# Products of nothing ahead of the first join of four groups, in a fused RWKV-7 and top-k expert kernel

## The chip, the cores and the metric

The kernel runs on one core of a Trainium2 chip. Its time is the device time of one execution in microseconds (us); the figure given for a kernel is the median of several executions. The profile is of one execution; its span runs from the first to the last instruction on the core.

## What is computed

An RWKV-7 recurrence over 768 steps, for 4 batches of 8 heads of width 40, and behind it a mixture of 8 experts that keeps the best 80 tokens of each expert.

```python
for t in range(S):                                    # S = 768
    y[:, :, t] = np.einsum('bhd,bhde->bhe', rt, state)
    Sa = np.einsum('bhde,bhe->bhd', state, at)
    state_decay = state * wt[:, :, None, :] - np.einsum('bhd,bhe->bhde', Sa, bt)
    state = state_decay + np.einsum('bhd,bhe->bhde', vt, kt)
# x: (3072, 320) from y
logits = x @ w_gate                                   # 8 experts
# each expert keeps its `capacity` = 80 tokens of the largest gate weight
h = np.maximum(x[tok_idx] @ w1[e], 0.0)
out[tok_idx] = gate_w[tok_idx, None] * (h @ w2[e])
```

## The kernel before

The 768 steps are cut into 12 chunks of 64, and the batches into 2 pairs: 24 units of work. A unit is prepared (`prepare`: loads, transposes, running products, scores), its triangular system is inverted, and it is finished (`finish`: the values, the state update, the output rows). Units 0 to 3 are inverted on TensorE by repeated squaring (`doubling`). From unit 4 on four units form a group, `batches[1]` to `batches[5]`: units 4 to 7, 8 to 11, 12 to 15, 16 to 19, 20 to 23. `invert` writes a group's scores to DRAM (`blocks`), fetches them into a layout in which GpSimd (POOL) solves all the 32-row diagonal blocks of the group at once (lines 677 and 679, 30 steps), writes the solutions and their transposes back (`solved`, `flipped`, line 697), and SyncE (SP) loads these into the tiles `d1` (line 706), `nt` (line 713) and `d0` (line 719).

`solve` joins the 32-row blocks of one unit to 64-row blocks with two sets of eight small products on TensorE: `g_go` multiplies `nt` and `d0` (line 737; called G below), ScalarE (ACT) copies the result to `gt` (line 742), `x_go` multiplies `gt` and `d1` (line 752; called X), and ACT copies that back into `nt` (line 757). G of the first unit of a group waits for that group's loads.

After that the unit's `finish` runs: `u_go` (line 875) and `ut_go` (line 894) on TensorE, copies on ACT (880, 900), the masked product `lam` (line 811, masked on VectorE, DVE, at line 818 into `UL`), then the large products of `keys_go` (line 930) that give state and output. `gate` works out the gate weights of a group, writes rows to DRAM (`x_rows`, line 1048), turns the gate weights on TensorE (line 1063) and keeps the ten times eight largest so far with pairs of DVE instructions (lines 1056 and 1058, ten rounds).

The order of the work is written by a planner. Every operation is handed over with `add(engine, duration, lag, when, function, reads, writes, psum)`, and `Plan.order` lists all of them by a simulated clock; each engine then executes its own list strictly in that order. The planner also places the results of TensorE in the eight banks of PSUM (`bank(key)` gives the place). G is handed over as an operation of 0.6 us. A DMA of the hardware queues takes one of eight semaphores by turns, so one that is issued later can wait for an earlier one on its semaphore.

When all units are through, the 80 best are known, token numbers are worked out from them, the rows are gathered and the experts run in six passes (`first_layer`, `second_layer`). In that part there are already products of nothing, `keep_warm` at line 1173, seven of 384 columns.

Of the kernel before, what the change touches and what calls it, by code (L numbers as in the profile page):

```python
# [17 lines left out]
class Plan:  # L18
# [7 lines left out]
    def add(self, eng, us, lag, when, fn, reads=(), writes=(), psum=None, to=()):  # L26
        whole = eng == "PE" and psum[0][0] in WHOLE
        o = dict(eng=eng, us=us, lag=lag, when=when, stage=self.stage, fn=fn, whole=whole, i=len(self.ops), deps=set(), psum=None,
                 reads=list(reads), writes=list(writes), to=list(to))
        if psum:  # L30
            key, n = psum
            if key not in self.width:
                self.width[key] = n
                o["psum"] = key
            o["writes"].append(key)
        o["kind"] = f"{eng} {(psum[0] if psum else [*o['writes'], *o['reads'], ('none', 0)][0])[0]}"
        for key in o["reads"]:
            for p, wrote in self.touch.get(key, ()):
                if wrote:
                    o["deps"].add(p)  # L40
        for key in o["writes"]:
            for p, _ in self.touch.get(key, ()):
                o["deps"].add(p)
        for key in o["reads"]:
            self.touch.setdefault(key, []).append((o["i"], False))
        for key in o["writes"]:
            self.touch.setdefault(key, []).append((o["i"], True))
        self.ops.append(o)
# [140 lines left out]
def kernel(  # L189
# [19 lines left out]
    nc = tc.nc  # L209
# [25 lines left out]
    batches = [list(range(n, n + GU)) for n in range(0, NM, GU)]  # L235
# [11 lines left out]
    ident = const.tile([128, 128], F32, name="ident")  # L247
# [25 lines left out]
    def view(t, offset, *dims):  # L273
        return bass.AP(t.tensor, t.offset + offset, [list(t.ap[0])] + [list(d) for d in dims])
# [28 lines left out]
    with ExitStack() as p1:  # L303
        hold = p1.enter_context(tc.tile_pool(name="hold", bufs=1))
        psp = p1.enter_context(tc.tile_pool(name="psp", bufs=1, space=PSUM))
        ps = psp.tile([128, 8, 512], F32, name="ps")
# [8 lines left out]
        begins = hold.tile([128, H * SEG], F32, name="begins")  # L315
# [13 lines left out]
        def at(name, n):  # L329
            return buf[name][n % RINGS[name]]  # L330

        def group(name, n):
            return wide[name][(n // GU) % WIDE[name]]

        def quads_of(name, n, rows=slice(0, 128)):
            return group(name, n)[rows].rearrange("p (q u i t) -> p u q i t", q=2, u=GU, t=T)[:, n % GU]

        def bank(key):
            return plan.home[key]
# [290 lines left out]
        def invert(kq):  # L630
# [93 lines left out]
            add("SP", 0.8 * 2 * len(qs), 2.6, z + 5, d0_go, [("flp", kq)], [("d0", n) for n in ns])  # L724
            add("SP", 0.8 * 2 * len(qs), 3.2, z + 5, nt_back_go, [("sol", kq)], [("nt", n) for n in ns])

        def solve(n):
            z = n * PER

            kg, kx = ("G", n), ("X", n)  # L730

            def g_go():
                b0 = bank(kg)
                nt, d0 = quads_of("nt", n), quads_of("d0", n)
                for i in range(M4):
                    for q in range(2):
                        nc.tensor.matmul(ps[HB * q : HB * q + HB, b0, T * i : T * i + T], lhsT=nt[:, q, i, :],
                                         rhs=d0[:, q, i, :], start=True, stop=True, skip_group_check=True)
            add("PE", 0.6, 0.3, z - 8, g_go, [("nt", n), ("d0", n)], (), (kg, 1), [("gt", n)])

            def gt_go():
                nc.scalar.copy(at("gt", n).rearrange("p (c t) -> p c t", t=T)[:, :, 0:C],
                               ps[:, bank(kg), 0:256].rearrange("p (c t) -> p c t", t=C))
            add("ACT", 0.4, 0.1, z - 7, gt_go, [kg], [("gt", n)])

            def x_go():
                b0 = bank(kx)
                gt = at("gt", n).rearrange("p (i x t) -> p i x t", x=2, t=T)
                d1 = group("d1", n).rearrange("p (u i x c) -> p u i x c", u=GU, x=2, c=T)[:, n % GU]
                for i in range(M4):  # L750
                    for x in range(2):
                        nc.tensor.matmul(ps[T * x : T * x + T, b0, T * i : T * i + T], lhsT=gt[:, i, x, :],
                                         rhs=d1[:, i, x, :], start=True, stop=True, skip_group_check=True)
            add("PE", 0.6, 0.3, z - 6, x_go, [("gt", n), ("d1", n)], (), (kx, 1), [("nt", n)])

            def tm_go():
                nc.scalar.copy(quads_of("nt", n)[:, :, :, C:],
                               view(ps[:, bank(kx), :], 0, (C, 2), (T, M4), (1, C)))
            add("ACT", 0.4, 0.1, z - 5, tm_go, [kx], [("nt", n)])
# [334 lines left out]
        for kq, ns in enumerate(batches):  # L1094
            plan.stage = (ns[-1] >= 2 * GU) + (ns[-1] == NM - 1)
            for n in ns:
                prepare(n)
            if kq:
                invert(kq)
            for n in ns:  # L1100
                if kq:
                    solve(n)
                finish(n)
                if n == groups[group_of[n]][-1]:
                    gate(group_of[n])
# [58 lines left out]
    with ExitStack() as p2:  # L1164
# [35 lines left out]
        for m0 in range(0, NM, CH):  # L1200
# [3 lines left out]
            for m in range(m0, m0 + CH):  # L1204
                nc.tensor.matmul(ip, lhsT=hot[:, m - m0, :], rhs=ids[:, m].rearrange("p i e -> p (i e)"),
                                 start=m == 0, stop=m == NM - 1)
# [3 lines left out]
        for i, n in enumerate((HB, C)):  # L1210
            for j in range(128 // n):
                nc.tensor.matmul(spread[n * j : n * j + n, i].rearrange("p i e -> p (i e)"),
                                 lhsT=ident[0:HW, HB * i : HB * i + n], rhs=i0, start=True, stop=True, skip_group_check=True)
# [133 lines left out]
```

## Time and profile before

| | us |
|---|---|
| median of 3 executions | 568.6 |
| lowest and highest | 563.7 and 569.66 |
| the profiled execution | 569.61 |
| its span | 567.5 |
| TensorE (PE) products busy / weights loading | 454.1 / 371.6 |
| VectorE (DVE) busy | 339.3 |
| GpSimd (POOL) busy | 222.8 |
| ScalarE (ACT) busy | 208.8 |
| mean granted clock of TensorE | 0.921 of full |

In the profile a line such as "L737" is a line of the kernel before. A row of the timeline gives the start and length in us of a run of equal instructions, its engine and line, what it writes and reads, and in brackets how long the engine stood idle ahead of it and what ended that. An fp32 product is two matmul instructions. PEclk is the clock that TensorE was granted, as a share of full speed.

The recurrence ends at about 467 us. The first joins of the five groups start at 167.6, 235.4, 303.1, 369.6 and 423.4 us.

### The profile page before, as it was taken

To read this page: it belongs to the slowest core of one execution; us is meant where nothing else is said; L and a number is where in the kernel's file an instruction comes from. 1 tells how busy PE (TensorE), PEld (TensorE's weight loads), DVE (VectorE), ACT (ScalarE), POOL (GpSimd) and SP (SyncE) were. 2 spreads that over 40 slices of the span, in tenths; PEclk is the share of its full clock that TensorE was granted. 3 is DMA by queue.
4 is the path that set the end of the run, shared out by engine and by line. 5 is a ranking of instruction groups with operands and counts; after the bars stand their busy time and mean duration, and the time that the engine had idled before them with its cause. 6 is when DMAs were issued, how large, how long until landed. Compare 5 with 4: busy or idle time off the path is not lost. (4 is left out here: it accounts for less than half of the span.)

```text
span 567.5 us, 28199 instructions
## 1 busy us (share of the span) xinstructions
PE 454.1 (80%) x12677; PEld 371.6 (65%) x12677; DVE 339.3 (60%) x752; ACT 208.8 (37%) x424; POOL 222.8 (39%) x412
## 2 busy tenths in 40 slices
PE   2868888689889998699985999399829860799996
PEld 2767777678778887588874988388828750434442
DVE  6879777265363895487663786374377688621211
ACT  1445465346533454245542455234314320021010
POOL 7000001895408982598404986388400000120101
PEclk9999999889987999789997899779968995599999
DMA  7645658433595658856687544832591539289600
GB/s 132 115 73 86 102 102 137 80 75 76 110 176 107 118 94 182 175 98 120 153 146 142 90 92 110 167 53 46 131 188 40 186 100 331 73 241 351 235 13 17
DMA packets 239392, 71.81 MB, mean 127 GB/s; under 512 B 216520, under 2 KB 233928, under 8 KB 239272
## 3 DMA queue, kind: packets, MB, share of 16 engines
q1 hardware_dynamic: 218360, 51.15, 45.5%
q10 hardware_dynamic: 18176, 9.19, 6.3%
q0 software_dynamic: 2736, 9.67, 5.1%
q8 instruction: 99, 1.62, 1.1%
q14 instruction: 21, 0.17, 0.1%
HBM read 52.11 MB, written 16.72 MB: 121 GB/s over the span
## 5 line engine op out<-in xcount | busy, mean ns | idle before, releaser
L677 POOL TENSOR_TENSOR tmp<-lt 128x30 f32<-128x30 f32 (+9 forms) x150 | 80.2, 534 | 34.5 <-DMA lt<-blocks 23.4
L679 POOL TENSOR_TENSOR lt<-lt,tmp 128x30 f32<-128x30 f32 (+9 forms) x150 | 86.6, 577 | 11.7
L661 POOL DMA_DIRECT2D lt<-blocks x5 | 2.9, 586 | 129.9 <-PE ps L437 79.9
L604 PE MATMUL ps<-slot,kbT 40*64 40x64 f32 x1536 | 34.7, 224 | 8.4 <-issue 4.9
L604 PEld LDWEIGHTS ps<-slot,kbT 40*64 40x64 f32 x1536 | 29.0, 136 | 12.1 <-issue 6.3
L543 DVE TENSOR_TENSOR_SCAN slot<-dec,begins 128x520 f32<-128x520 f32 x24 | 31.6, 1317 | 4.6 <-POOL cand L345 3.4
L930 PE MATMUL ps<-UL,slot 64*64 64x128 f32 x768 | 30.0, 293 | 2.3 <-DVE UL L818 1.9
L930 PE MATMUL ps<-VL,slot 64*64 64x128 f32 x768 | 27.8, 272 | 4.8 <-issue 4.7
L818 DVE TENSOR_TENSOR UL<-ps,mask 128x512 f32<-128x512 f32 x24 | 16.5, 688 | 24.8 <-PE ps L811 24.7
L551 DVE TENSOR_TENSOR_SCAN iv<-dec,ends 128x520 f32<-128x520 f32 x24 | 30.9, 1286 | 0.7
L973 DVE TENSOR_TENSOR xT<-ps,slot 128x512 f32<-128x512 f32 x24 | 16.5, 688 | 22.9 <-PE ps L930 22.9
L783 ACT COPY VL<-rawv 128x320 f32<-128x320 f32 x24 | 11.0, 459 | 50.3 <-PE ps L930 41.4
L437 PE MATMUL ps<-ident,slot 128*128 128x128 f32 x192 | 28.6, 297 | 0.9 <-issue 0.8
L593 ACT COPY kbT<-ps 128x1024 f32<-128x1024 f32 x24 | 24.4, 1015 | 13.3 <-PE ps L437 12.2
L1303 POOL DMA_INDIRECT out_dram<-y,idx_s x6 | 6.0, 994 | 57.3 <-DVE y L1302 57.3
L794 ACT COPY rv<-ps 128x1024 f32<-128x1024 f32 x24 | 24.3, 1013 | 10.7 <-PE ps L437 10.7
L1039 POOL TENSOR_TENSOR ids<-gsm,tok 128x32 bf16<-128x32 f32 (+1 forms) x14 | 3.0, 231 | 63.9 <-DVE gsm L1029 43.3
L624 DVE TENSOR_TENSOR slot<-ps,mask 128x512 f32<-128x512 f32 x24 | 16.4, 685 | 17.5 <-PE ps L604 17.5
L930 PEld LDWEIGHTS ps<-VL,slot 64*64 64x64 f32 x768 | 22.3, 135 | 6.8 <-issue 6.8
L985 PE MATMUL ps<-wsel,xT 128*128 128x88 f32 x192 | 25.8, 277 | 1.1 <-DVE xT L973 1.0
L930 PEld LDWEIGHTS ps<-UL,slot 64*64 64x64 f32 x768 | 23.3, 143 | 4.8 <-DVE UL L818 2.7
L985 PEld LDWEIGHTS ps<-wsel,xT 128*128 128x128 f32 x192 | 23.3, 191 | 2.5 <-DVE xT L973 1.5
(216 smaller groups left out, 1143.8 us busy)
## 6 DMA issues: line engine op xcount, KB each, us to landing
w<-in_moe_w_dram SPq DMA_DIRECT2D x4, 1280.0 KB
slot<-in_moe_w_dram SPq DMA_DIRECT2D x4, 1120.0 KB, 7.8
slot<-in_moe_w_dram SPq DMA_DIRECT2D x4, 1024.0 KB, 8.3
w<-in_moe_w_dram SPq DMA_DIRECT2D x4, 1024.0 KB, 11.9
x_rows<-xg ACTq DMA_DIRECT2D x24, 160.5 KB, 3.5
rawk<-in_k_dram SPq DMA_DIRECT2D x48, 80.0 KB, 3.0
raww<-in_w_dram SPq DMA_DIRECT2D x48, 80.0 KB, 3.1
rawr<-in_r_dram SPq DMA_DIRECT2D x48, 80.0 KB, 3.0
```

The costliest lines, as they stand in the source:

```text
L437: nc.tensor.matmul(o, lhsT=i, rhs=ident, start=True, stop=True, is_transpose=True, skip_group_check=True)
L543: nc.vector.tensor_tensor_scan(at("P", n), at("dec", n)[:, 0 : H * SEG], begins, 0.0, op0=Alu.mult, op1=Alu.add)
L551: nc.vector.tensor_tensor_scan(at("iv", n)[:, H * SEG : 0 : -1], at("dec", n)[:, H * SEG : 0 : -1], at("ends", n)[:, H * SEG : 0 : -1], 0. ...
L593: nc.scalar.copy(at("kbT", n).rearrange("p (k c) -> p k c", k=2), ps[:, bank(kk) : bank(kk) + 2, :])
L604: nc.tensor.matmul(ps[T * o : T * o + T, b0 + q, T * i : T * i + T], lhsT=at("kbT", n)[rows, 512 * x + c : 512 * x + c + T], rhs=at("ah", ...
L677: e.tensor_tensor(out=tv, in0=t3[:, 0:s, s : s + 1].to_broadcast([np_, s, n]), in1=t3[:, s : s + 1, s + 1 :].to_broadcast([np_, s, n]), op ...
L679: e.tensor_tensor(out=t3[:, 0:s, s + 1 :], in0=t3[:, 0:s, s + 1 :], in1=tv, op=Alu.add)
L794: nc.scalar.copy(at("rv", n).rearrange("p (k c) -> p k c", k=2), ps[:, bank(kr) : bank(kr) + 2, :])
L818: nc.vector.tensor_tensor(out=view(at(name, n), 512, (HB, 2), (2 * HB, 4), (1, T)), in0=view(ps[:, bank(key), :], 0, (512, 2), (T, 4), (1, ...
L930: nc.tensor.matmul(ps[HB * q : HB * q + HB, b0 + bb, 128 * i : 128 * i + 128], lhsT=at("kb", n)[rows, o : o + HB], rhs=view(at(name, n)[ro ...
L973: nc.vector.tensor_tensor(out=view(at("xT", n), 0, (T, 2), (128, M4), (1, T)), in0=view(ps[:, bank(ky), :], HB, (512, 2), (128, M4), (1, T ...
L985: nc.tensor.matmul(ps[:, b0, o : o + 88], lhsT=at("xT", n)[:, 128 * i : 128 * i + 128], rhs=wsel[:, i, :], start=True, stop=True, skip_gro ...
```

## The change

Ahead of the first G of the groups `batches[2]` to `batches[5]` (units 8, 12, 16 and 20) the kernel issues 3, 6, 10 and 8 products of 512 columns. Each multiplies the identity by the first 512 columns of the constant tile `begins` (zeros, with a one in every 65th column) and writes the bank that this G then overwrites. They are inside `g_go`, so the planner does not know of them and its order stays.

```diff
+        FILL = {batches[2][0]: 3, batches[3][0]: 6, batches[4][0]: 10, batches[5][0]: 8}
+
         def solve(n):
...
             def g_go():
                 b0 = bank(kg)
+                for _ in range(FILL.get(n, 0)):
+                    nc.tensor.matmul(ps[:, b0, :], lhsT=ident, rhs=begins[:, 0:512], start=True, stop=True, skip_group_check=True)
                 nt, d0 = quads_of("nt", n), quads_of("d0", n)
```

## The prediction

> **What bounds the kernel now.** I read the share of busy time first (TensorE 454 of 567.5 us), then TensorE's list of waits (us in total, times, longest), since the change touches nothing else.
>
> ```profile
> PE ps L737 <- DMA d<-flipped: 18.9, 3, 9.7
> PE thr_p L1180 <- DVE thw L1178: 11.9, 1, 11.9
> PE ps L737 <- DMA d<-solved: 8.2, 1, 8.2
> ```
>
> Two of TensorE's three longest waits are G, the line ahead of which the products go: 18.9 + 8.2 = 27.1 us in four waits. The timeline of TensorE gives the four places:
>
> ```profile
> 235.44 1.12 PE L737 MATMUL ps<-d,spare_nt 128*64 128x64 f32 x16 [3.26 <-DMA d<-flipped]
> 303.07 1.12 PE L737 MATMUL ps<-d,nt 128*64 128x64 f32 x16 [5.94 <-DMA d<-flipped]
> 369.58 1.12 PE L737 MATMUL ps<-d,spare_nt 128*64 128x64 f32 x16 [9.68 <-DMA d<-flipped]
> 423.42 1.12 PE L737 MATMUL ps<-d,nt 128*64 128x64 f32 x16 [8.16 <-DMA d<-solved]
> 425.00 1.19 PE L752 MATMUL ps<-d,gt 128*64 128x64 f32 x16
> 429.70 0.69 PE L752 MATMUL ps<-d,gt 128*64 128x64 f32 x16
> ```
>
> These are units 8, 12, 16 and 20. The last two rows are the same work, X, five us apart: 1.19 us and 0.69 us. The clock explains it, in the view of chosen windows (bounds, length, busy us and count of PE, PEld, DVE, ACT, POOL, then PEclk, DMA share, GB/s):
>
> ```profile
> 235.30:245.30 10.00, 8.17 (x167) 7.12 (x169) 3.76 (x12) 1.95 (x6) 8.62 (x18) 0.50 0.83 160
> 300.10:306.80 6.70, 3.73 (x38) 3.31 (x40) 1.39 (x6) 1.17 (x3) 2.29 (x9) 0.50 0.78 122
> 307.00:310.00 3.00, 2.60 (x117) 2.16 (x113) 0.93 (x2) 0.50 (x2) 2.53 (x7) 1.00 0.53 115
> 361.60:375.10 13.50, 5.46 (x115) 4.81 (x116) 4.34 (x19) 1.54 (x4) 9.60 (x24) 0.50 0.81 158
> 416.20:429.70 13.50, 6.19 (x117) 5.14 (x117) 10.50 (x37) 1.97 (x5) 0.00 (x0) 0.50 0.73 126
> ```
>
> The clock falls to half in or just behind each wait and stays there after G has begun: until about 245.4, 306.9, 375.2 and 429.8. So each group pays twice: for the wait, which the products don't shorten, and for 10.0, 3.8, 5.6 and 6.4 us of half speed behind it. The loop of a group is a chain of latencies through TensorE (POOL itself waits for `blocks` 50.1 us in all), so time gained behind a join is passed on: the loads of the next group are issued behind work that TensorE paces.
>
> [...] only 0.50 and 1.00 stand in windows inside a state, and the stretches above are about 10.2, 6.8, 13.7 and 13.7 us long[...]. [...] The products here are plain ones of the identity with a mostly zero operand; the kernel has such products already, at L1173:
>
> ```profile
> 491.40:494.50 3.10, 3.10 (x13) 1.85 (x10) 2.43 (x15) 0.00 (x0) 1.07 (x1) 0.50 0.00 0
> 494.80:497.20 2.40, 2.35 (x8) 1.08 (x6) 0.00 (x0) 0.09 (x1) 1.95 (x2) 1.00 0.51 137
> ```
>
> Nothing else ran on TensorE from 491.5 to 494.6, and the clock rose[...].
>
> **The change part by part.** *Cost of a product.* The groups by line give the length of one matmul, least first:
>
> ```profile
> L1173 PE MATMUL idle<-at,ident x14: 486/589/1009, 486.5 to 496.7; 128*128 128x384 f32 x14
> L1270 PE MATMUL hp<-slot,xe x64: 592/592/643, 498.5 to 518.6; 128*64 128x512 f32 x32, 128*32 128x512 f32 x32
> ```
>
> At full clock 128 columns more cost 592 - 486 = 106 ns, 0.83 ns a column; 512 columns occupy 0.425 us. A product is two instructions: 0.85 us at full clock, 1.70 at half. So 3, 6, 10 and 8 products take 2.55, 5.1, 8.5 and 6.8 us.
>
> *Do they fit?* They wait only for the last reader of their bank. By the program's semaphores that is ACT's copy L846 for unit 8 (ended 231.5), an older copy L539 for unit 12, DVE's L862 for unit 16 (359.10 + 0.49 = 359.6), nothing for unit 20. So they start when TensorE falls idle: about 232.0, 297.1, 359.8 and 415.2, and end at 234.6, 302.2, 368.3 and 422.0, ahead of G by 0.8, 0.9, 1.3 and 1.4 us. Added cost at full clock: nothing, hidden in the wait. [...]
>
> *What is gained.* Warm, the first G takes 0.62 us to the next instruction instead of 1.05 (262.79 to 263.41 against 423.42 to 424.47), X the same, L875 0.49 instead of 0.87, L894 about 0.6 instead of 1.03. By group, following the queue:
>
> - Unit 8: G and L604 behind it would be 0.9 us faster, but X then waits for `d1`, whose first two loads had landed and the others landed at about 239.5. The idle time that this leaves (236.8 to 239.6) is 2.8 us[...]. I take 0; at most 1.3 us (UL at DVE L818 waited 0.64 us for TensorE, and the rounds of DVE ahead of it would start 0.7 earlier).
> - Unit 12: 0.43 of G, 0.86 of the eight transposes behind it (304.13 to 306.02, warm 1.03). ACT's copies and the issue of `x_rows`, for which the next `gt` waits, move along. 1.2 us, at least 0.3 if that issue is held by its DMAs.
> - Unit 16: TensorE alone would gain 2.0. But `d1` landed at 371.05, so X starts no earlier than that; and DVE has eight rounds of gate weights ahead of UL:
>
> ```profile
> 371.15 0.29 DVE L1066 COPY cand<-ps 128x128 f32<-128x128 f32 x1 [8.75 <-PE ps L1063]
> 377.22 0.69 DVE L818 TENSOR_TENSOR UL<-ps,mask 128x512 f32<-128x512 f32 x1 [0.48 <-PE ps L811]
> ```
>
> UL waited for TensorE only 0.48 us, and the rounds start 0.58 us earlier (G 0.43, the transpose L1063 0.15). DVE is late next: 1.06 us.
> - Unit 20: the transpose L1071 behind G waits for DVE's rounds, which end at 424.4 whatever TensorE does; from there L1071, X (`d1` landed at 424.8), L1077, G, L875 and L894 run warm: X of unit 21 at about 427.5 instead of 429.70. DVE's UL waited 1.17 us and the rounds ahead of it start 0.8 earlier: 1.97 at most. I take 1.9.
>
> The sum is 0 + 1.2 + 1.06 + 1.9 = 4.2 us. The other engines' lists are unchanged. At the end of the recurrence DVE's last rounds and TensorE are a near tie (the gate reduction at 468.31 follows the tenth round), but these rounds are themselves started by TensorE's earlier unit, so the gain passes.
>
> **To the time.** The profiled execution took 569.6 us: 569.6 - 4.2 = 565.4. It lies 1.0 above the median of 568.6, so for a median I say 564.4.
>
> **The rivals.**
>
> *Everything comes back.* Unit 8 also stays warm and neither DVE nor `d1` binds. Half-speed work behind the joins, at 42% saved: about 5.8, 3.8, 5.6 and 6.4 us, 21.6 x 0.42 = 9.0, so 559.6. [...] Against it: DVE's 0.48 us of slack at unit 16 is in a fixed order.
>
> *The clock falls anyway.* The remaining gaps of 0.8 to 1.4 us, the wait for `d1` and the DVE wait that replaces the old one [...] drop the clock again a little later. For it: a gap of 1.84 us at 309.7 to 311.6, [...] was followed by half clock from 313.7 to 317.1. Against it: gaps of about 1.1 us (273.4, 411.7) were not. It gives 568 to 568.6.
>
> *Products that outlast the wait (slower).* If the clock is half when they begin, a product takes 1.70 us. [...] The point from which it decides is 0.8 to 1.4 us of lost work, that is 1.6 to 2.8 us at half clock. [...] If the clock never rose, 5.1, 10.2, 17.0 and 13.6 us against waits of 3.3, 5.9, 9.7 and 8.2 would add 18.8: 587.4.
>
> **How the numbers follow.** The forecast gets 0.53, everything back 0.13, the clock that falls anyway 0.22, products that outlast 0.12. The forecast's own range is 562.5 to 567 (2 to 6 us of gain). The three executions before spread over 6 us, so the range reaches to the first rival below and takes in the second: 559.5 to 569.5. About 1% is what a measurement of this kernel can tell from no change. Faster by more than that means below 562.9: most of the first rival and the lower edge of the forecast, 0.22. Slower means above 574.3, the tail of the last rival: 0.06. The rest, 0.72.
>
> **What would show it.** In the changed profile TensorE's waits ahead of G shrink to about 1 us each, and PEclk reads 1.00 where it was 0.50 behind units 12, 16 and 20; G there takes 0.69 us instead of 1.12. Behind unit 16 UL waits for DVE's own rounds and TensorE for UL by about 1 us. Unit 8 keeps a stretch at half clock behind its wait for `d1`. The forecast is wrong if G starts straight behind its last product (they outlast the load), if the distance between the first joins of two groups does not shrink by 1 us or more from unit 12 on, or if half clock merely moves.

## The result, and the profile after

| | before | after |
|---|---|---|
| median of 22 executions each, us | 567.37 | 570.42 |
| lowest and highest | 561.14 and 574.9 | 565.14 and 579.35 |
| the profiled execution / its span | 569.61 / 567.5 | 569.11 / 567.0 |
| mean granted clock | 0.921 | 0.940 |

Ratio after to before 1.0075, 95% interval 1.0047 to 1.0102: slower by 0.75% in this set of runs, where a gain of 4.2 us was forecast. The ratios given here compare, for each kernel, only those runs that lie within 1.5% of its own fastest; as the runs of one kernel spread over 2 to 3%, what that leaves out depends on their number, so I set the difference of the plain means over all runs beside it, with its standard error (here +3.5 +- 1.1 us).

Nothing in the profile looks slower at first. In the page of the changed kernel (engine, busy us, share, instructions; then the clock in tenths by slices of 14.2 us; then a DMA queue with packets, MB and share):

```profile
PE 476.3 (84%) x12731; PEld 380.8 (67%) x12731; DVE 341.7 (60%) x752; ACT 208.6 (37%) x424; POOL 223.6 (39%) x412
PEclk9999999899988998999998999999999875599999
q8 instruction: 100, 1.64, 1.2%
```

The 22 us by which TensorE is busier are the products, and the clock is higher (0.940 against 0.921). The line numbers of the changed kernel are 4 higher from G on: the products are L737, G is L741, `lam` L815 with its mask at L822, `keys_go` L934, the turn of the gate weights L1093. TensorE's timeline at the four joins:

```profile
230.01 2.74 PE L737 MATMUL ps<-begins,ident 128*128 128x512 f32 x6
234.09 0.69 PE L741 MATMUL ps<-d,spare_nt 128*64 128x64 f32 x16 [1.34 <-DMA d<-flipped]
...
294.01 5.42 PE L737 MATMUL ps<-begins,ident 128*128 128x512 f32 x12
299.36 0.69 PE L741 MATMUL ps<-d,nt 128*64 128x64 f32 x16
...
364.34 0.69 PE L741 MATMUL ps<-d,spare_nt 128*64 128x64 f32 x16 [1.30 <-DMA d<-flipped]
...
415.94 0.69 PE L741 MATMUL ps<-d,nt 128*64 128x64 f32 x16 [0.83 <-DMA d<-solved]
```

This is what the prediction promised. The waits of 3.3, 5.9, 9.7 and 8.2 us have become 1.3, none, 1.3 and 0.8, every G takes 0.69 us, and from unit 8's G to unit 20's it is 181.9 us (415.94 - 234.09) instead of 188.0. Unit 20's G starts 7.5 us earlier than before (2.6 of these were there at unit 4 already, ahead of the change). At the end of the span 0.5 us of them is left. The list of waits (us in total, times, longest) has one kind that the prediction did not price:

```profile
PE ps L934 <- issue: 7.3, 6, 2.7
PE ps L947 <- issue: 3.2, 2, 1.7
PE ps L741 <- DMA d<-flipped: 2.6, 2, 1.3
PE ps L815 <- issue: 2.6, 1, 2.6
PE ps L741 <- DMA d<-solved: 0.8, 1, 0.8
```

The list of before has it too, for instance in this row (L930 is the changed kernel's L934):

```profile
PE ps L930 <- issue: 5.0, 4, 2.4
```

"issue" is time in which TensorE had no operand to wait for. In all it is not more than before (26.2 against 27.1 us); what changed is where it falls. Behind the last join the changed kernel has two stops of over 2.5 us (2.70 and 2.58), where before has one of 2.42. The timeline of TensorE and of DVE, first before:

```profile
454.98 0.77 PE L930 MATMUL ps<-VL,slot 64*64 64x128 f32 x19 [2.42 <-issue]
461.30 0.67 DVE L818 TENSOR_TENSOR UL<-ps,mask 128x512 f32<-128x512 f32 x1
464.39 0.21 PE L943 MATMUL ps<-rv,sT 40*64 40x64 f32 x1 [1.04 <-issue]
470.44 0.38 PE L1089 MATMUL ps<-ident,gates 128*8 128x128 f32 x2 [3.00 <-DVE gates L1034]
```

Then after:

```profile
436.10 0.33 PE L934 MATMUL ps<-UL,slot 64*64 64x128 f32 x2 [2.70 <-issue]
458.52 0.49 PE L815 MATMUL ps<-rv,uT 40*64 40x64 f32 x7 [2.58 <-issue]
459.14 0.69 DVE L822 TENSOR_TENSOR UL<-ps,mask 128x512 f32<-128x512 f32 x1 [2.80 <-PE ps L815]
468.94 0.59 PE L1093 MATMUL ps<-ident,gates 128*8 128x128 f32 x2 [3.00 <-DVE gates L1038]
```

The last `UL` is the mark. Before, DVE took it up without a wait, so the stop of 2.42 us had been made good; after, DVE stands 2.80 us for `lam`, which is broken in two by a stop (25 matmul instructions, then seven at 458.52). And the clock, which had been full there, falls. The chosen windows (bounds, length, busy us and count of PE, PEld, DVE, ACT, POOL, then PEclk, DMA share, GB/s), one row of before and three of after:

```profile
429.90:470.60 40.70, 31.00 (x1072) 27.75 (x1070) 31.44 (x94) 13.13 (x32) 0.78 (x4) 1.00 0.44 130
```

```profile
436.10:444.00 7.90, 7.90 (x164) 7.51 (x165) 3.21 (x10) 2.39 (x7) 0.39 (x2) 0.57 0.33 94
444.10:457.60 13.50, 9.91 (x349) 8.45 (x348) 8.65 (x25) 3.43 (x8) 0.00 (x0) 1.00 0.54 165
457.60:464.60 7.00, 4.61 (x87) 4.02 (x86) 4.30 (x11) 0.00 (x0) 0.00 (x0) 0.51 0.02 4
```

From unit 20's G to the last turn of the gate weights ("the last stretch" below) before took 470.44 - 423.42 = 47.0 us, after 468.94 - 415.94 = 53.0. That is where 6 of the 7.5 us went; 1.0 more went between that turn and the first expert product (28.1 and 29.1 us), which I did not follow up. Of the 6, the stops for issue account for 2.6 (6.5 us in the stretch against 3.9). The other 3.4 go with the clock, which was at half for 14.8 us of the stretch instead of 6.3; how much of them the half clock cost is not measured.

**Where the stops come from.** The queue q8 ("instruction" in the page) brought 99 packets before and 100 after, 1.64 MB: 16.4 KB each. The trace of the changed kernel has 12,731 matmuls, as many weight loads and 146 other TensorE instructions, 25,608 in all: 256 to a packet. So I take each packet to bring TensorE a block of 256 instructions. Half a block's instructions are matmuls, so block ends should come every 128 matmuls. They do: in every trace of this case in which weights are loaded early, the stops for issue of over 1 us behind the last join fall at the same place of the count of TensorE's matmuls, modulo 128 (35 or 36): ahead of them stand 11556 and 12067 matmuls after (and 11811 at a stop of 0.83 us), 11811 and 12067 before. Not every block comes in time: of the 26.2 us that TensorE stood for issue, 23.0 end 2 to 3 us behind the beginning of a q8 packet, and one stop took 2.7 us. In most of the last stretch a packet begins some 10 to 80 matmuls into a block, so that the next one is there in time, and at full clock two packets are 3.4 to 4.5 us apart. The packet that ends the stop at 436.10 began at 433.68, 7.2 us behind the one ahead of it, when TensorE had already used up its block, and as a transfer of early weights of 1,120 KB, issued at 428.1, came to its end; so did the one at 456.22, 6.8 us behind its predecessor, with 1,120 KB issued at 451.0. In each case TensorE went on some 2.4 us after the packet began.

The change's 27 products add 54 matmuls and 54 weight loads ahead of the tail. That moves which matmul a block begins with. This is theory A: the loss is the place of the block ends in the last stretch, under bursts of weights, not the time of the products.

### The profile page after: what moved, and what is told of

It reads as the page before. It is cut to its first block, busy times and chain, and to the rows that moved or that the text cites. A ratio compares the mean times of both kernels' runs of the same rounds, so it can differ in the third digit from the quotient of the medians.

```text
span 567.0 us, 28307 instructions
## 1 busy us (share of the span) xinstructions
PE 476.3 (84%) x12731; PEld 380.8 (67%) x12731; DVE 341.7 (60%) x752; ACT 208.6 (37%) x424; POOL 223.6 (39%) x412
## 3 DMA queue, kind: packets, MB, share of 16 engines
q8 instruction: 100, 1.64, 1.2%
## 5 line engine op out<-in xcount | busy, mean ns | idle before, releaser
L677 POOL TENSOR_TENSOR tmp<-lt 128x30 f32<-128x30 f32 (+9 forms) x150 | 84.4, 562 | 33.8 <-DMA lt<-blocks 22.7
L679 POOL TENSOR_TENSOR lt<-lt,tmp 128x30 f32<-128x30 f32 (+9 forms) x150 | 82.8, 552 | 11.8
L934 PE MATMUL ps<-UL,slot 64*64 64x128 f32 x768 | 30.1, 287 | 7.6 <-issue 5.4
L543 DVE TENSOR_TENSOR_SCAN slot<-dec,begins 128x520 f32<-128x520 f32 x24 | 33.7, 1404 | 4.6 <-POOL cand L345 3.1
L604 PEld LDWEIGHTS ps<-slot,kbT 40*64 40x64 f32 x1536 | 29.1, 139 | 10.8 <-issue 4.7
L822 DVE TENSOR_TENSOR UL<-ps,mask 128x512 f32<-128x512 f32 x24 | 16.5, 689 | 25.2 <-PE ps L815 24.9
L934 PE MATMUL ps<-VL,slot 64*64 64x128 f32 x768 | 30.0, 285 | 1.9 <-issue 1.9
L934 PEld LDWEIGHTS ps<-UL,slot 64*64 64x64 f32 x768 | 23.2, 141 | 10.8 <-issue 7.0
L1043 POOL TENSOR_TENSOR ids<-gsm,tok 128x32 bf16<-128x32 f32 (+1 forms) x14 | 3.0, 233 | 66.8 <-DVE gsm L1033 42.5
L624 DVE TENSOR_TENSOR slot<-ps,mask 128x512 f32<-128x512 f32 x24 | 16.5, 686 | 17.1 <-PE ps L604 17.1
L934 PEld LDWEIGHTS ps<-VL,slot 64*64 64x64 f32 x768 | 24.1, 142 | 2.6 <-issue 2.4
L947 PE MATMUL ps<-rv,sT 40*64 40x64 f32 x768 | 23.1, 226 | 3.2 <-issue 3.2
```

The source lines that it names most:

```text
L543: nc.vector.tensor_tensor_scan(at("P", n), at("dec", n)[:, 0 : H * SEG], begins, 0.0, op0=Alu.mult, op1=Alu.add)
L604: nc.tensor.matmul(ps[T * o : T * o + T, b0 + q, T * i : T * i + T], lhsT=at("kbT", n)[rows, 512 * x + c : 512 * x + c + T], rhs=at("ah", ...
L624: nc.vector.tensor_tensor(out=at("psi", n).rearrange("p (q i t) -> p q i t", q=2, t=T), in0=quads(kp).rearrange("p q (i t) -> p q i t", t= ...
L677: e.tensor_tensor(out=tv, in0=t3[:, 0:s, s : s + 1].to_broadcast([np_, s, n]), in1=t3[:, s : s + 1, s + 1 :].to_broadcast([np_, s, n]), op ...
L679: e.tensor_tensor(out=t3[:, 0:s, s + 1 :], in0=t3[:, 0:s, s + 1 :], in1=tv, op=Alu.add)
L934: nc.tensor.matmul(ps[HB * q : HB * q + HB, b0 + bb, 128 * i : 128 * i + 128], lhsT=at("kb", n)[rows, o : o + HB], rhs=view(at(name, n)[ro ...
```

## The experiments

In the expectations, theory A is this one; the rivals are described in each (C is not the same in all of them). Times of kernels are compared only within one set of runs, in which before was timed too.

**Instructions without work, at the start.** Small bf16 products (about 30 ns each) ahead of everything else:

```diff
+        for _ in range(54):            # pad54; 64 in pad64, 128 in pad128; 74 and 10 ahead of the changed kernel
+            nc.tensor.matmul(ps[0:32, 7, 0:32], lhsT=ones_b[:, 0:32], rhs=ones_b[:, 0:32], start=True, stop=True, skip_group_check=True)
```

`pad54` is before with the change's 108 instructions; `after_pad74` is the changed kernel brought to 148 + 108 = 256.

> The kernel before with 54 small bf16 products (108 instructions, as many as the change adds) at the very start, where TensorE still waits for its first loads; none ahead of a join. Theory A (the change moves the places at which TensorE stops for its next block of 256 instructions, at 433.4 and 455.9 us for 2.7 and 2.6 us in the changed kernel, and there the clock falls): the late part of the list has the same shift as with the change, so these stops come at the same instructions and the time is 0.4 to 1.2% over before. Theory B (the products themselves cost: they outlast the loads, or their work lowers the clock later): no difference, within 0.2%. Theory C (the gain arrives and is lost at the end to the weights' transfers, because the end comes earlier): no difference, within 0.2%.

> The changed kernel with 74 small bf16 products at the start: 148 instructions and the 108 of the change are 256, one whole block, so behind the last group the blocks end at the same instructions as in the kernel before. Theory A: the gain of the joins shows, 0.5 to 1.3% faster than before. Theory B: 0.5 to 1.0% slower than before, as the changed kernel. Theory C: 0.3 to 1.0% slower, as the changed kernel.

`pad54`: 581.82 us against 573.82 of before, ratio 1.0155 (1.0057 to 1.0253). `after_pad74`: 573.50, ratio 0.9976 (0.9929 to 1.0024), so its difference to before is gone, the last stretch takes 47.1 us again and its stops are before's (2.22 and 1.31 us, both at before's products). The places of the stops are for A; the gain of 0.5 to 1.3% that A wanted on top is not there. And `pad54` lost more than the change itself, so three further kernels were to control it: one whole block, half a block, and half a block with the change.

> The kernel before with 128 small bf16 products (256 instructions, one whole block) at the start. In the trace of the run with 54 such products TensorE was through with them at 2.9 us, ahead of its first loads at 7.2. Theory A (what counts is where blocks of 256 instructions end): the ends lie where they lie before, so within 0.4% of before, and stops of over 0.6 us fall at the same products. A rival (such products at the start cost by themselves, a warmer clock early or a later start): slower by 1.5% or more, as 54 of them were.

> The kernel before with 64 small products (128 instructions, half a block) at the start. It is the base for the next kernel; theory A says only that it differs from before, between 0.5% faster and 1.6% slower, with its stops half a block away from those of before.

> The changed kernel with 10 small products at the start: 20 and 108 instructions, again half a block, so behind the last group the blocks end as in the kernel with 64. Theory A with a gain of its own in the joins: 0.4 to 1.0% faster than the kernel with 64 small products. Theory D (the joins' waits are set by transfers, the warm clock only makes the next wait longer, no gain of its own): within 0.2% of it.

> The changed kernel once more, beside the others on this chip: 0.5 to 1.0% slower than before, as measured; it ties this chip to the first comparison. Against the kernel with 54 small products, at the same ends of blocks behind the last group (1.0155 of before): 0.4 to 1.0% faster by theory A with a gain of its own, equal by theory D.

Against before at 573.60: `pad128` 580.42 and `pad64` 580.59 (four runs each: +4.7 +- 3.6 and +6.7 +- 2.6 us), `after_pad10` 574.67 (20 runs, 1.0067, 1.0019 to 1.0115; by plain means +0.6 +- 1.2), the changed kernel again 575.98 (four runs, +1.3 +- 2.0). `after_pad10` lies 6.1 +- 2.5 us below `pad64`, at the same block ends: for a gain of the products' own, and against rival D, but on four runs of `pad64`. `pad128` is a miss for A, which had it within 0.4% of before: its two longest stops are where before has them, but the last stretch takes 51.1 us and the median is 1.2% higher, though four runs that lie between 568.72 and 583.51 cannot tell its time from before's. Whether padding at the start has a price of its own in the first 170 us I did not settle: unit 4's G starts at 172.3 to 175.0 us in before with padding (`pad54`, `pad64`, `pad128`) and at 167.6 in before, but kernels untouched there show 165.0 to 175.6. It is a poor control, because it moves every block of the kernel, so I moved it to the place of the change.

**The same instructions inside a wait.** 54 small products (1.5 us in the trace) inside the 9.7 us wait ahead of unit 16's G of the kernel before, and 128 (one block, 3.5 us and a stop of 0.6):

```diff
+        TINY = {batches[4][0]: 54}     # tail108, tail108_b; 128 in tail256
...
                 b0 = bank(kg)
+                for _ in range(TINY.get(n, 0)):
+                    nc.tensor.matmul(ps[0:32, b0, 0:32], lhsT=ones_b[:, 0:32], rhs=ones_b[:, 0:32], start=True, stop=True, skip_group_check=True)
```

> The kernel before, with 54 small bf16 products (128x32 by 128x32 into 32x32, about 30 ns each, 1.6 us in all) in the 9.7 us wait ahead of G of unit 16: the change's 108 TensorE instructions, without its busy time. Nothing stands at the start. Theory A (the count of TensorE instructions decides where its blocks of 256 end in the tail): the stretch from G of unit 20 to the last gates transposition takes 52 to 57 us instead of 47, with stops ended by issue at the same products as in the changed kernel, and the time is 3 to 8 us (0.6 to 1.3%) above the kernel before. Rival B (the loss is the price of the products' busy time or of what they do to the clock, the blocks are a bystander): within 0.3% of the kernel before, that stretch 47 us.

> The kernel before, with 128 of the same small products at the same place: 256 TensorE instructions, one whole block, some 3.8 us inside a wait of 9.7. Theory A: block ends fall behind the last group at the same products as in the kernel before; that stretch takes 47 to 51 us and the time is within 0.4% of the kernel before (of the two with small products this is the faster one by 3 to 8 us). Rival B: both the same as before. Rival C (more instructions of any count cost, by fetch or by a busy array): slower than with 108, by over 1 us.

> The kernel before with 54 small products (108 TensorE instructions, 1.6 us inside the 9.7 us wait ahead of G of unit 16), timed again beside the next kernel, since it had 6 runs only. Theory A (block ends in the tail): over all its runs 2 to 6 us above the kernel before, the last stretch 50 to 55 us. Rival E (a chance of single profiles; in time the place of the block ends is worth nothing): within 1 us of the kernel before over all runs, and the last stretch anywhere from 45 to 53 us.

| | runs | median, before beside it | ratio (95%) | plain means, us | last stretch, us |
|---|---|---|---|---|---|
| tail108 | 6 | 578.29, 576.89 | 1.0115 (1.0037 to 1.0194) | +1.8 +- 1.3 | 50.3 |
| tail108_b | 22 | 579.8, 576.83 | 1.0031 (0.9989 to 1.0073) | +3.2 +- 1.0 | 52.9 |
| tail256 | 20 | 573.87, 576.89 | 1.0014 (0.9984 to 1.0045) | -2.1 +- 0.8 | 48.0 |

108 instructions that do nothing, hidden in a wait, cost 2.7 +- 0.8 us by plain means (both sets, weighted); 256 of them cost nothing. In the set that has both, `tail108` lies 3.9 +- 1.4 us above `tail256`. More work is faster than less, and of the explanations here only the place of the block ends has that: rivals B (the products' busy time) and C (any instruction costs) fall. The interval of `tail108_b` includes no change; its plain means and the profile carry it. And A does not say why `tail256` lies 2.1 us below before: an error of that size in such a difference has to be reckoned with. Timeline of TensorE and DVE in `tail108_b`:

```profile
448.54 0.33 PE L934 MATMUL ps<-UL,slot 64*64 64x128 f32 x2 [2.47 <-issue]
468.55 0.49 PE L815 MATMUL ps<-rv,uT 40*64 40x64 f32 x7 [2.85 <-issue]
469.17 0.69 DVE L822 TENSOR_TENSOR UL<-ps,mask 128x512 f32<-128x512 f32 x1 [3.07 <-PE ps L815]
```

and in `tail256`:

```profile
456.95 0.77 PE L934 MATMUL ps<-VL,slot 64*64 64x128 f32 x19 [1.64 <-issue]
463.27 0.67 DVE L822 TENSOR_TENSOR UL<-ps,mask 128x512 f32<-128x512 f32 x1
```

The first has the changed kernel's rows, down to the count of matmuls behind each stop (two, seven), without one of the changed kernel's products. The second has those of before (19), and DVE doesn't wait for the last `UL`. The first profile of the same kernel, `tail108`, is an exception:

```profile
468.54 0.67 DVE L822 TENSOR_TENSOR UL<-ps,mask 128x512 f32<-128x512 f32 x1
```

It has stops of 2.11 and 1.39 us in the stretch, both in `keys_go`, but none in `lam`, and its 50.3 us are short of the 52 to 57 that A wanted. Over all profiles DVE waits 2.4 to 3.4 us for the last `UL` in seven of the eight with half a block or the change's 108 instructions added, and not at all in the five with none or a whole block and in the three without bursts (below).

**The change with its block ends put back.** 3, 6, 7 and 8 products, and 80 small ones ahead of the seven: 256 instructions more than before in all.

```diff
-        FILL = {batches[2][0]: 3, batches[3][0]: 6, batches[4][0]: 10, batches[5][0]: 8}
+        FILL = {batches[2][0]: 3, batches[3][0]: 6, batches[4][0]: 7, batches[5][0]: 8}
+        TINY = {batches[4][0]: 80}
```

> The changed kernel with 3, 6, 7 and 8 products instead of 3, 6, 10 and 8, and 80 small ones ahead of the seven: 48 + 160 + 48 = 256 instructions more than before in all, the small ones about as long together as the three products that they replace. Theory A: the gain at the joins stays (G of unit 20 some 5 us earlier counted from G of unit 4), the block ends fall as in the kernel before, the last stretch takes 47 to 49 us: 2 to 6 us (0.4 to 1.0%) faster than before and over 1% faster than the changed kernel. Rival D (what is gained ahead of unit 20 is always lost again behind it, whatever the block ends): the last stretch takes 52 us or more, time as the changed kernel.

> The changed kernel itself again, beside the other three on one chip. Every theory: 0.5 to 1.0% slower than the kernel before. Theory A: the last stretch takes 52 to 53 us with stops ended by issue of 2 us or more at two products. If the clock's edges alone decided, that stretch would differ between executions of the same program by as much as between the kernels.

On one chip, before at 576.89: `after_even` 572.99, ratio 0.9979 (0.9943 to 1.0016), plain means -2.5 +- 0.9; the changed kernel 575.52, ratio 1.0039 (1.0004 to 1.0075), -0.4 +- 0.9. The even one is 2.1 +- 1.1 us faster than the changed kernel (573.9 and 576.0 on average), with a last stretch of 45.6 against 51.4 us, and its stops are before's: 

```profile
457.57 0.77 PE L938 MATMUL ps<-VL,slot 64*64 64x128 f32 x19 [1.67 <-issue]
466.98 0.21 PE L951 MATMUL ps<-rv,sT 40*64 40x64 f32 x1 [1.04 <-issue]
```

That is against rival D. The changed kernel itself was to be 0.5 to 1.0% slower than before by every theory and is not, by plain means (0.4% by the ratio). The promised "over 1% faster than the changed kernel" was missed (0.4%), and so was the gain at the joins: from unit 4's G to unit 20's it took 256.4 us, not some 5 less than before's 255.8. Its 16 matmuls ahead of unit 20's G took 8.54 us, 0.53 us each, where the 20 ahead of unit 16's G in the changed kernel took 8.85, 0.44 each, at a clock of 1.00; I estimate from these two that some 3 us of the 8.54 passed at half clock. No wait for the load is left behind them. That is the slower rival's case, at one place.

**No bursts.** Of the four early experts `FIRST` have their weights loaded behind the recurrence's last rows. The other two have theirs issued as soon as tiles come free, in before at 409 to 457 us: these are the bursts. At 4 none are left.

```diff
-    EARLY, FIRST = 4, 2
+    EARLY, FIRST = 4, 4
```

> The kernel before with all four early experts' weights loaded behind the recurrence (FIRST = 4 instead of 2), so that no weights move while units 20 to 23 run. All theories: the stops of TensorE for instructions behind 420 us get shorter (2.4 us at 452.6 before); the weights come later, which may cost up to 10 us at the experts. It is the base for the next kernel.

> The changed kernel with the same hold. Against the kernel before with the hold, theory A: 0.5 to 1.3% faster, since stops are short wherever they fall. Theory B: 0.5 to 1.0% slower. Theory C: 0.5 to 1.3% faster.

> The changed kernel with its instructions brought to 256 more than before (3, 6, 7 and 8 products and 80 small ones), and all four early experts' weights loaded behind the recurrence, so that no burst of weights is on the DMA engines while the last block of TensorE's instructions is fetched. Theory A: no stop ended by issue over 1.7 us in the tail, the last stretch 42 to 46 us, of which the weights' late arrival takes back 3 to 4 us behind it; 3 to 6 us below the kernel before (0.5 to 1.0%). Rival E: the bursts do not matter, the late weights alone do: 2 to 4 us slower than the even kernel with its bursts, so as the kernel before.

`before_hold` 569.56 and `after_hold` 570.25 against 573.82 of before: ratios 1.004 (0.9991 to 1.0089) and 0.9947 (0.9911 to 0.9984); by plain means -2.4 +- 1.1 and -3.4 +- 0.9. A wanted the second 0.5 to 1.3% below the first; that is open, as it is 0.9% by these ratios and -1.1 +- 1.2 us (0.2%) by plain means. `after_even_hold` 574.12 against 576.83, 0.9956 (0.9908 to 1.0004), -2.3 +- 1.0: just short of what A wanted (3 to 6 us), and level with the even kernel with its bursts. With the bursts away q8's packets in `after_hold` come 3.5 to 4.3 us apart behind unit 20's G, and of TensorE's stops for issue these two are the longest that its timeline has between 418 and 470 us:

```profile
431.68 0.46 PE L815 MATMUL ps<-rv,uT 40*64 40x64 f32 x15 [0.21 <-issue]
455.17 0.43 PE L861 MATMUL ps<-st,slot 40*64 40x40 f32 x14 [0.21 <-issue]
```

So behind the last join the burst is the second condition for the stop: the last stretch takes 43.8 us (before), 42.5 (change) and 41.8 (even), wherever the blocks end. In before the stops in it fall from 3.9 to 0.2 us, and the stretch by 3.3. Elsewhere other transfers do the same: in `before_hold` a stop of 1.89 us ends at 222.51, with no weights on their way but 312 GB/s moved in the 4 us ahead of its packet. The weights then come late: from the last turn of the gate weights to the first expert product 31.1, 31.9 and 30.8 us instead of 28.0, 29.0 and 27.9, and 65.4 instead of 63.7 from there to the end of the last one. Some 4.7 us are given back.

All profiles together, by instructions added ahead of the tail (modulo 256):

| added | last stretch, us | stops for issue in it, us | half clock in it, us |
|---|---|---|---|
| 0 (before, pad128, tail256, after_pad74, after_even) | 47.1, 51.1, 48.0, 47.1, 45.6 | 3.9, 5.3, 3.4, 3.9, 3.8 | 6.3, 13.6, 13.9, 8.3, 0 |
| 108 (after, after_again, after_third, pad54, tail108, tail108_b) | 53.2, 52.0, 51.4, 56.9, 50.3, 52.9 | 6.5, 6.3, 5.9, 5.4, 3.5, 6.8 | 14.8, 14.4, 14.0, 29.6, 16.1, 15.3 |
| 128 (pad64, after_pad10) | 51.3, 49.7 | 5.5, 4.4 | 17.1, 11.8 |
| no bursts: 0, 108, 256 | 43.8, 42.5, 41.8 | 0.2, 0.4, 0.2 | 9.7, 2.1, 3.1 |

(These count from the first instruction of each trace to the start of the last single turn, so they can differ by 0.2 us from differences of the rows above.) The first two rows have means of 47.8 and 52.8 us, and one kernel in each reaches into the other. Of these 5.0 us the stops themselves make 1.7 (4.1 and 5.7 on average); the rest goes with the half clock, 8.4 and 17.4 us. So the larger part of the loss goes with the slow clock and not with the standing still itself. Behind the last join all profiles together have 16 stops of over 2 us; at 11 of them half clock set in during the stop or within 1.1 us of its end. That a stop set off the other stretches of half clock is not shown. Where the clock's changes fall can be part of that scatter: counted from the span's start they lie on 3.09 us plus multiples of 3.413 us in before, on 0.29 plus such multiples in after. But three profiles of the changed kernel lie within 2 us, so that does not decide alone.

**The fastest** against before is `after_hold` (0.9947; the interval excludes 1). It was not run beside the changed kernel; by their ratios to before (0.9947 and 1.0075) it is about 1.3% below it.

## Why the prediction was wrong

- *Products hidden in the wait, G behind a short rest of it:* right, at 1.3, 0, 1.3 and 0.8 us. At unit 12 nothing is left, a first sign named for failure, but G came no later: 65.3 us behind unit 8's, against 67.6.
- *Clock:* right. Behind units 16 and 20 it read 1.00 until 437.2, behind 12 until 307.5; unit 8 kept a half-speed stretch (239.2 to 242.6).
- *DVE late next behind unit 16:* near. `UL` came 6.7 us behind G instead of 7.6, a gain of 0.9 where 1.06 was said, and still waited 0.17 us for TensorE.
- *The sum of the gains, 4.2 us:* mis-sized. In this one profile the distances of the first joins shrank by 2.4, 1.5 and 2.2 us where 0, 1.2 and 1.06 were said, and unit 20's 1.9 did not show, as the last stretch grew. That the first three came out above the forecast is luck: over all profiles, G of unit 8 to G of unit 20 takes 186.7 us on average with the products (eight kernels) and 187.2 without (eight). Where the block ends or the bursts are matched, the products gain 0.4 +- 1.1 (`after_even` against `tail256`), 0.6 +- 1.0 (`after_pad74` against before) and 1.1 +- 1.2 us (`after_hold` against `before_hold`): 0.7 +- 0.6 together, of 4.2 forecast. Only the last stretch is some 1.5 us shorter at equal block ends, near the 1.9 taken for unit 20. The half clock behind units 12 and 16 was priced as if one profile's half-clock stretches were those of every execution, and the 0 for unit 8 was the author's estimate. What takes the time instead in these groups is open.
- *"Added cost at full clock: nothing, hidden in the wait":* this is the step that failed, and turned the sign. The products' time was hidden; their number was not. 108 instructions cost 2.7 +- 0.8 us (`tail108`, `tail108_b`) without one of the products.
- *"The other engines' lists are unchanged ... so the gain passes":* the lists were unchanged, but TensorE's own list arrives in blocks (100 packets for 25,608 instructions), and the near tie of DVE and TensorE at the end was decided in this profile by a stop in `lam`, ahead of DVE's last `UL`. None of the rivals had this.

Together: -0.7 + 2.7 = +2.0 us, against +3.5 +- 1.1 in the runs that gave the result, and +1.2 +- 0.7 when the changed kernel's three timed sets (+3.5, +1.3, -0.4) are weighted together. So part of the +3.5 is probably chance, and the sign of the last set shows how near to nothing the change is; that the same program stands at +0.6% in one set and at nothing in another is left open.

## What to carry to other kernels

Where an engine runs through tens of thousands of unrolled instructions, as TensorE does here (25,608, in blocks of 256), count the instructions that an edit adds, not their time alone: read the "issue" waits, find their place in the count of instructions modulo a block, and ask which product the next blocks will begin with and what big transfers run as they are fetched. To try an edit for its own worth, pad it to a whole block and put the padding into a wait next to it, not at the start. A gain read from one profile's half-clock stretches is a gain of that execution (here 0.7 +- 0.6 us came of the 4.2), so price it from several before adding it up.

## What the runs showed of the hardware

- TensorE's instruction packets came late under transfers of 1.0 to 1.1 MB on q1. At the stops of over 2 us behind the last join two packets were 6.0 to 7.3 us apart instead of 3.4 to 4.5, and 306 to 333 GB/s had been moved in the 4 us ahead of the late one (194 at one stop); the stops were up to 3.2 us long. From the packet's begin to the next matmul it was 2.3 to 2.8 us each time.
- In the last stretch of before and after a packet began in the block just ahead of the one that it brings, not earlier: some 10 to 80 matmuls into it as a rule, and with its 128 used up at the stops of over 2 us.
- Of the 16 stops of over 2 us behind the last join, the seven of 2.58 to 3.17 us were all followed by half clock, and of the nine of 2.07 to 2.47 us four: 2.17 (`after_again`) and 2.30 us (`after_third`) were, 2.42 (before) and 2.47 us (`tail108_b`) were not. The length alone does not decide.
- TensorE's granted clock was 0.50 or 1.00 in the profiles of before and after, and each stretch between two of its changes is 3.41 us or a whole multiple of it: at half clock from 230 us on 10.24, 6.83, 3.41, 13.65, 13.65 and 23.89 us in before, 3.41, 3.41, 6.83, 6.83 and 27.31 us in after.
- 54 small products (108 instructions) cost more than 128 of the same (256 instructions), by 3.9 +- 1.4 us in one set of runs.
- The first 165.0 to 175.6 us, up to unit 4's G, differ by 10 us between profiles of kernels that have the same work there. That is more than any edit here moved, and no profile of one execution can be set against another without that stretch being taken off first.
